# Moving a denominator row into the first of seven matrix products, and two products and two weight loads forward

## The chip, the cores and the metric

The kernel runs on one core of one Trainium2 chip. The metric is the device time of one execution in microseconds (us); lower is better. A core has TensorE (matrix products; PE in the profile, its weight loads PEld), VectorE (DVE), ScalarE (ACT) and GpSimd (POOL), each with an instruction queue of its own, and SyncE (SP), whose queue here issues the transfers (DMA) between the large memory (HBM) and the on-chip memory (SBUF). Matrix products land in PSUM, of which this kernel uses eight banks of 128 x 512 float32. Engines wait for one another by semaphores, which the kernel's framework derives from what each instruction reads and writes.

## The reference

Four layers, each with a residual: linear attention (A), a gated product (B), and both again with the same weights. S is 2048, D is 1024, 32 heads of 32.

```python
def _A_ref(x, wqkv, wo):
    qkv = (x @ wqkv) ...                       # q, k, v by head
    phi = lambda t: jnp.where(t > 0, t + 1, jnp.exp(t)) + 1e-6
    pq, pk = phi(q), phi(k)
    kv = jnp.einsum("bhsd,bhse->bhde", pk, v)
    z = jnp.einsum("bhsd->bhd", pk)            # sum of phi(k) over the sequence
    num = jnp.einsum("bhqd,bhde->bhqe", pq, kv)
    den = jnp.einsum("bhqd,bhd->bhq", pq, z)[..., None] + 1e-6
    o = num / den
    return o ... @ wo

x = x + _A_ref(_layernorm(x), A_wqkv, A_wo)    # layer 0
x = x + _B_ref(_layernorm(x), ...)             # layer 1
x = x + _A_ref(_layernorm(x), A_wqkv, A_wo)    # layer 2: the change is here
x = x + _B_ref(_layernorm(x), ...)             # layer 3
```

## The kernel before

Only the second attention (layer 2) is concerned. The kernel never forms v. It takes M = xn^T phi(k), a 1024 x 1024 product over the sequence (xn is the normalised x), and then kv = Wv^T M by head. M is done with seven products of blocks of half the size instead of eight (a Strassen-like scheme), each of four groups of eight matmuls, one group to a PSUM bank. X, Y and V are the banks; `done(j)` follows group j.

```python
def m_products(q_first):
    X = [self.ps.tile([P, NW], F32, tag="a", ...) for j in range(QT)]     # four banks
    Y = [self.ps3.tile([P, NW], F32, tag="b", ...) for j in range(2)]     # two banks
    Y += [self.kvp.tile([P, NW], F32, tag=f"kv{j}", ...) for j in range(2)]   # kv0, kv1
    mt, V, M5 = [], [], []

    def product(A, B, banks, start, done):
        for j in range(QT):
            for i in range(NS):
                nc.tensor.matmul(banks[j], lhsT=A(i)[:, j * P:(j + 1) * P], rhs=B(i), ...)
            done(j)
            later.tick()
    ...
    def add(out, j):                                     # VectorE
        nc.vector.tensor_tensor(out=out, in0=Y[j], in1=M5[j], op=ALU.add)

    product(..., X, True, lambda j: copy(Y[j], X[j]))    # 1: X, copied to Y by ScalarE
    mt += [self.slot(f"mt{l}_{h}", [P, 4, D]) for h in range(2)]
    product(..., X, False, evict(X, 0, 0))               # 2: X ends
    z_row()
    later.at(2, lambda: z_chain(0))
    V += [self.ps.tile([P, NW], F32, tag="a", ...) for j in range(QT)]
    for i in range(NS):
        later.at(1 + i // 2, lambda i=i: sums_last(i))
    product(..., V, True, keep)                          # 3
    product(..., Y, False, lambda j: add(V[j], j))       # 4: V starts from Y + M5
    product(..., V, False, evict(V, 0, 1))               # 5
    product(..., Y, False, lambda j: add(half(mt[1][:, j, :], 1), j))   # 6: M's second half
    kv.extend(self.ps.tile([P, NW], F32, tag="a", ...) for i in range(H))

    def steps(h, b):                                     # 16 matmuls of kv[b]
        for j in range(QT):
            kv_half(h * QT + j, mt[h][:, j, :], b)

    def last(j):
        copy(half(mt[1][:, j, :], 0), Y[j])
        if j < 3:
            steps(*((0, 1), (1, 1), (0, 0))[j])
        if j == 1:
            ring.load_to(ring.index((l, "o0")) + 1)      # half of wo

    product(..., Y, False, last)                         # 7
    q_first()
    later.tick()
    steps(1, 0)
    ring.load_to(ring.index((l, "o1")) + 1)              # other half of wo
    finish_kv()                                          # kv[0] by VectorE, kv[1] by ScalarE
# (cut: operands of the products)
```

`sums_last` makes, on VectorE, two in-place differences per row block (sixteen in all) which products 5 and 7 read, and which may be written only once product 2 has read the old values. The denominator: GpSimd sums phi(k) over row blocks into `ksum`; a matmul with ones then sums over the 128 rows (`z_row`); and each of sixteen row blocks of phi(q) is divided, by GpSimd and VectorE in turn:

```python
def z_row():
    hi = self.temp([P, D], BF16)
    nc.scalar.activation(out=hi, in_=ksum, func=ACT.Copy)
    for i in range(H):
        ps = self.ps.tile([P, NW], F32, tag="a")
        nc.tensor.matmul(ps, lhsT=self.ones, rhs=hi[:, i * NW:(i + 1) * NW], start=True, stop=True)
        nc.scalar.activation(out=zrow[:, i * NW:(i + 1) * NW], in_=ps, func=ACT.Copy)

def z_chain(i):
    z_mult(*divmod(i, QT))
    if i < 10:
        later.at(2, lambda: z_chain(i + 1))

def z_mult(sc, j):
    prod = ksum                                          # the one buffer of all products
    nc.gpsimd.tensor_tensor(out=prod, in0=pq_of[sc, j], in1=zrow, op=ALU.mult)
    later.at(2, lambda: z_sum(prod, sc, j))

def z_sum(prod, sc, j):
    nc.vector.tensor_reduce(out=den, in_=heads(prod), ...)
    nc.vector.tensor_scalar(out=den, in0=den, scalar1=1e-6, ...)
    nc.vector.reciprocal(out=den, in_=den)
    later.at(2, lambda: z_scale(den, sc, j))

def z_scale(den, sc, j):
    nc.gpsimd.tensor_tensor(out=heads(pq), in0=heads(pq), in1=den ..., op=ALU.mult)
    self.last_turn = nc.sync.dma_start_transpose(out=pqT[sc][:, :, j * P:(j + 1) * P], in_=pq)
# (cut)
```

`later.at(n, f)` runs f, that is, puts its instructions into the queues, n ticks later; a tick is a group or a unit of TensorE's work. `ring` is the list of weight tiles in order of use; `load_to` issues loads up to one of them, into a buffer that the pool has free. Weights, phi(q), its transposes and M's parts share one pool of sixteen buffers. After the products come the last quarter of q (units of eight matmuls, with phi by ScalarE and VectorE), four times `fold_wo` between them (kv times half of wo, which gives T), and the output units, T times the transposed phi(q).

Of the kernel before, what the change touches and what calls it, by code (L numbers as in the profile page):

```python
# [9 lines left out]
ACT = mybir.ActivationFunctionType  # L10
F32 = mybir.dt.float32
BF16 = mybir.dt.bfloat16
F16 = mybir.dt.float16
PSUM = bass.MemoryType.PSUM
P = 128
NW = 512
# [73 lines left out]
class _Net:  # L90
# [318 lines left out]
    def layer_A(self, l, last_ln):  # L409
        nc, G, KT, D = self.nc, self.G, self.KT, self.D  # L410
        ring, later = self.ring, self.later
        H = D // NW
        heads = lambda a: a.rearrange("p (h d) -> p h d", d=HD)
        pq_of, pqT, T = {}, {}, []
        kv = [] if l else [self.kvp.tile([P, NW], F32, tag=f"kv{i}", name=f"kv{l}_{i}")
                           for i in range(H)]
        kvc = self.slot(f"kvc{l}", [P, 4, D])
# [2 lines left out]
        ksum = kvc[:, 2:4, :].rearrange("p a d -> p (a d)").bitcast(F32)  # L420
# [33 lines left out]
            else:  # L454
                nc.gpsimd.tensor_tensor(out=ksum[:, cols], in0=ksum[:, cols], in1=pk, op=ALU.add)  # L455

        def z_row():

            hi = self.temp([P, D], BF16)
            nc.scalar.activation(out=hi, in_=ksum, func=ACT.Copy)  # L460
            for i in range(H):
                ps = self.ps.tile([P, NW], F32, tag="a")
                nc.tensor.matmul(ps, lhsT=self.ones, rhs=hi[:, i * NW:(i + 1) * NW],
                                 start=True, stop=True)
                nc.scalar.activation(out=zrow[:, i * NW:(i + 1) * NW], in_=ps, func=ACT.Copy)
# [17 lines left out]
        def kv_half(d, mt, b):  # L483
            for i in range(NW // P):
                nc.tensor.matmul(kv[b][:, i * P:(i + 1) * P].rearrange("p (i d) -> p i d", d=HD),
                                 lhsT=ring.get((l, f"v{b}"))[:, d, i * P:(i + 1) * P],
                                 rhs=by_row(mt[:, b * NW:(b + 1) * NW])[:, :, i, :], start=(d == 0 and i == 0),
                                 stop=(d == KT - 1 and i == NW // P - 1),
                                 skip_group_check=True)
# [8 lines left out]
        half = lambda a, n: a[:, n * NW:(n + 1) * NW]  # L498
# [16 lines left out]
        def sums_last(i):  # L515
            a, b = self.xn[l, self.NS + i], self.pk[l, self.NS + i]
            sub(half(a, 0).bitcast(F16), half(a, 0), part(i, 1))
            sub(half(b, 0).bitcast(F16), half(b, 0), part(i, 3))

        def m_products(q_first):  # L520

            NS = self.NS
            xn, pk = (lambda i: self.xn[l, i]), (lambda i: self.pk[l, i])
            f16 = lambda a: a.bitcast(F16)
            copy = lambda out, src: nc.scalar.activation(out=out, in_=src, func=ACT.Copy)
            X = [self.ps.tile([P, NW], F32, tag="a", name=f"mx{j}") for j in range(QT)]
            Y = [self.ps3.tile([P, NW], F32, tag="b", name=f"my{j}") for j in range(2)]
            Y += [self.kvp.tile([P, NW], F32, tag=f"kv{j}", name=f"my{2 + j}") for j in range(2)]
            mt, V, M5 = [], [], []

            def product(A, B, banks, start, done):
                for j in range(QT):
                    for i in range(NS):
                        nc.tensor.matmul(banks[j], lhsT=A(i)[:, j * P:(j + 1) * P], rhs=B(i),
                                         start=start and i == 0, stop=i == NS - 1,
                                         skip_group_check=True)
                    done(j)
                    later.tick()

            def evict(banks, h, n):  # L540
                return lambda j: copy(half(mt[h][:, j, :], n), banks[j])

            def keep(j):
                M5.append(self.temp(name="m5"))
                copy(M5[j], V[j])

            def add(out, j):
                nc.vector.tensor_tensor(out=out, in0=Y[j], in1=M5[j], op=ALU.add)

            product(lambda i: half(xn(i), 0), lambda i: half(pk(i), 0), X, True,  # L550
                    lambda j: copy(Y[j], X[j]))
            mt += [self.slot(f"mt{l}_{h}", [P, 4, D]) for h in range(2)]
            product(lambda i: half(xn(NS + i), 0), lambda i: half(pk(NS + i), 0), X, False,
                    evict(X, 0, 0))
            z_row()
            later.at(2, lambda: z_chain(0))
            V += [self.ps.tile([P, NW], F32, tag="a", name=f"mv{j}") for j in range(QT)]
            for i in range(NS):
                later.at(1 + i // 2, lambda i=i: sums_last(i))
            product(lambda i: part(i, 0), lambda i: part(i, 2), V, True, keep)  # L560
            product(lambda i: part(i, 1), lambda i: part(i, 3), Y, False, lambda j: add(V[j], j))
            product(lambda i: f16(half(xn(NS + i), 0)), lambda i: half(pk(NS + i), 1), V, False,
                    evict(V, 0, 1))
            product(lambda i: f16(half(xn(i), 1)), lambda i: f16(half(pk(i), 1)), Y, False,
                    lambda j: add(half(mt[1][:, j, :], 1), j))
            kv.extend(self.ps.tile([P, NW], F32, tag="a", name=f"kv{l}_{i}") for i in range(H))

            def steps(h, b):
                for j in range(QT):
                    kv_half(h * QT + j, mt[h][:, j, :], b)  # L570

            def last(j):
                copy(half(mt[1][:, j, :], 0), Y[j])
                if j < 3:
                    steps(*((0, 1), (1, 1), (0, 0))[j])
                if j == 1:
                    ring.load_to(ring.index((l, "o0")) + 1)

            product(lambda i: half(xn(NS + i), 1), lambda i: f16(half(pk(NS + i), 0)), Y, False, last)
            q_first()  # L580
            later.tick()
            steps(1, 0)
            ring.load_to(ring.index((l, "o1")) + 1)
            finish_kv()

        def finish_kv():
            n = NW // P
            nc.vector.tensor_copy(out=kvT[:, 0:n, :].rearrange("p g e -> p (g e)"), in_=kv[0])
            nc.scalar.activation(out=kvT[:, n:2 * n, :].rearrange("p g e -> p (g e)"), in_=kv[1],
                                 func=ACT.Copy)  # L590
# [12 lines left out]
# [6 lines that stand above are left out]
            prod = ksum  # L609
            nc.gpsimd.tensor_tensor(out=prod, in0=pq_of[sc, j], in1=zrow, op=ALU.mult)  # L610
            later.at(2, lambda: z_sum(prod, sc, j))
# [70 lines left out]
        if l == 0:  # L682
            steps = self.head()
# [29 lines left out]
        with self.tc.manual_schedule(engines={mybir.EngineType.DVE, mybir.EngineType.Pool}):  # L713
            q3 = row_major(q_unit, self.NQ - 1)
            out0 = column_major(out_unit, 0)
            if l == 0:
                ring.free_before((l, "v0"))
                later.at(5, z_row)
                later.at(7, lambda: z_chain(0))
                for d in range(KT):  # L720
                    m_units(d)
            else:
                ring.load_to(ring.index((l, "v1")) + 1)
                m_products(q3.pop(0))
                q3.insert(0, lambda: None)
                later.at(1, lambda: self.behind(ring.last, self.bring_back, range(self.NS)))
                for t in range(self.NS, self.ST, 2):
                    later.at(10 + t, lambda t=t: self.behind(self.last_turn, self.bring_back, (t, t + 1)))
# [334 lines left out]
```

## Time and profile before

| what | value |
|---|---|
| time, median of 3 runs | 1488.01 us (1485.56 to 1488.08) |
| span of the profiled execution | 1483.2 us |
| granted TensorE clock, mean | 0.999 |
| products 1 to 7 of layer 2, TensorE | 841.33 to about 894.8 us from the span's start |
| last quarter of q and the folds | about 893 to 916.8 us |
| output units of layer 2 | about 914.8 to 972 us |

A row of the profile's groups names the source line, the engine, the operation, what it writes and reads, and its times. L534 is a matmul of a product, L463 the matmul with ones, L485 one of kv, L641 of a fold, L436 of a projection, L656 of an output unit. On VectorE, L500 is a difference, L548 the sum `add`, L615 to L617 the reduce, the added 1e-6 and the reciprocal of a denominator, L383 and L385 phi, L588 the copy of kv[0], L650 a copy of a fold. On GpSimd, L455 is the sum into `ksum`, L610 the multiply of a denominator, L622 its scale. On ScalarE, L460 is the copy of `ksum`, L465 that of the row. In a view in order of time the columns are start and duration in us, engine, line, operation, output and inputs, and the count of merged instructions; what stands in brackets is how long the engine had been idle before it, and what ended that.

### The profile page before, as it was taken

How to read it: one execution, taken by the hardware profiler on the slowest of the kernel's cores; microseconds unless marked ns; L12 is line 12 of the kernel's file. 1: busy time of each engine (PE TensorE's matmuls, PEld its weight loads, DVE VectorE, ACT ScalarE, POOL GpSimd, SP SyncE). 2: the span in 40 equal slices, each digit the busy share in tenths (PEclk: the TensorE clock that was granted, in tenths of full speed). 3: DMA queues.
4: the chain of work that ended last, by engine and by line, in shares of the span. 5: the costliest groups of instructions: out<-in, count | busy, mean ns of one | idle time of the engine just before them, and what ended most of it. 6: DMA issues, size and time to landing. Idle time of an engine off the chain costs nothing.

```text
span 1483.2 us, 18604 instructions
## 1 busy us (share of the span) xinstructions
PE 1468.9 (99%) x6965; PEld 667.1 (45%) x7007; DVE 873.1 (59%) x1495; ACT 512.8 (35%) x919; POOL 284.0 (19%) x190
## 2 busy tenths in 40 slices
PE   9999999999999999999999998999999999999999
PEld 4444444444444444444444444444444444444444
DVE  8995787666594434455379867874445433434632
ACT  5752323333330333340067523343333203333300
POOL 1356540111100011110023485401111000111000
PEclk9999999999999999999999999999999999999999
DMA  9855538444458954446833029894444688444461
GB/s 280 220 167 177 114 59 246 156 143 156 161 185 251 338 179 131 148 131 199 251 100 71 1 39 293 213 279 142 138 145 131 187 244 268 142 142 146 150 209 43
DMA packets 316059, 251.32 MB, mean 169 GB/s; under 512 B 105536, under 2 KB 291136, under 8 KB 315072
## 3 DMA queue, kind: packets, MB, share of 16 engines
q1 hardware_dynamic: 306000, 229.80, 52.6%
q10 hardware_dynamic: 9968, 20.32, 3.7%
q8 instruction: 55, 0.90, 0.3%
q14 instruction: 36, 0.29, 0.1%
HBM read 190.84 MB, written 34.60 MB: 152 GB/s over the span
## 4 chain that ended last, share of the span: by engine, by line
PE 91%; DVE 6%; POOL 2%; DMA 1%; issue 1%; ACT 0%; DVEq 0%
PE ps L436 14%; PE yg L850 10%; PE dy L934 10%; PE yu L850 10%; PE dv L934 6%; PE dx L934 6%; PE xg L850 6%; PE xu L850 6%; PE ps L473 4%; PE vg L850 3%; PE vu L850 3%; PE zu L850 3%; PE zg L850 3%; PE ps L656 3%; DVE x L663 1%; DVE stats L154 1%
## 5 line engine op out<-in xcount | busy, mean ns | idle before, releaser
L850 PEld LDWEIGHTS <-w 128*128 128x128 f16 (+1 forms) x3136 | 306.3, 98 | 371.3 <-DVE w L788 1.1
L888 POOL TENSOR_TENSOR h<-m5u,m5g 128x512 f16<-128x512 f32 x56 | 71.2, 1271 | 812.1 <-DVE m5u L884 801.2
L436 PE MATMUL ps<-w,xnT 128*128 128x512 bf16 x1024 | 224.8, 381 | 0.2 <-ACT xnT L296 0.2
L934 PEld LDWEIGHTS <-h 128*128 128x128 f16 x1120 | 109.4, 98 | 132.3
L881 DVE TENSOR_TENSOR zg<-yg,m5g 128x512 f32<-128x512 f32 x56 | 39.2, 699 | 203.5 <-PE yg L850 203.5
L436 PEld LDWEIGHTS <-xnT 128*128 128x128 bf16 x1024 | 99.6, 98 | 121.3 <-issue 3.5
L850 PE MATMUL yg<-s,w 128*128 128x512 f16 x448 | 115.2, 380 | 0.0
L850 PE MATMUL xu<-xnT,w 128*128 128x512 f16 x448 | 115.0, 380 | 0.0
L850 PE MATMUL xg<-xnT,w 128*128 128x512 f16 x448 | 115.0, 380 | 0.0
L850 PE MATMUL yu<-s,w 128*128 128x512 f16 x448 | 115.0, 380 | 0.0
L656 PE MATMUL ps<-T,pqT 128*128 128x512 bf16 x500 | 110.5, 380 | 2.7 <-DVE x L663 2.1
L858 ACT ACTIVATE m5g<-m5g 128x512 f32<-128x512 f32 x56 | 35.2, 629 | 200.2 <-DVE m5g L884 200.2
L934 PE MATMUL dy<-w,h 128*128 128x512 f16 x448 | 98.0, 380 | 0.0
L934 PE MATMUL dx<-w,h 128*128 128x512 bf16 x436 | 96.7, 379 | 0.6
L610 POOL TENSOR_TENSOR kvc<-pq,kvc 128x1024 f32<-128x1024 bf16 x32 | 70.4, 2200 | 71.9 <-DVE den L615 57.7
L656 PEld LDWEIGHTS <-pqT 128*128 128x128 bf16 x512 | 49.9, 98 | 62.9 <-issue 3.1
L154 DVE BATCH_NORM_STATS2 stats<-x 128x6 f32<-128x512 f32 (+1 forms) x120 | 76.6, 672 | 0.5 <-DMA x<-in_A_x_dram 0.3
L161 ACT ACTIVATE rstd<-mv,eps 128x1 f32<-128x1 f32 x64 | 18.1, 289 | 162.2 <-DVE mv L159 162.1
L455 POOL TENSOR_TENSOR kvc<-kvc,slab 128x512 f32<-128x512 f32 x46 | 58.3, 1273 | 73.7 <-DVE slab L385 56.0
L861 DVE TENSOR_TENSOR h<-yu,r 128x512 f16<-128x512 f32 x56 | 38.7, 691 | 56.6 <-PE yu L850 56.6
L884 DVE TENSOR_TENSOR m5u<-yu,m5u 128x512 f32<-128x512 f32 x56 | 38.7, 692 | 54.0 <-PE yu L850 54.0
L934 PEld LDWEIGHTS <-e 128*128 128x128 f16 x448 | 43.8, 98 | 52.9
(127 smaller groups left out, 1969.6 us busy)
## 6 DMA issues: line engine op xcount, KB each, us to landing
w<-in_B_W_gate_dram SPq DMA_DIRECT2D x56, 512.0 KB, 6.0
w<-in_B_W_up_dram SPq DMA_DIRECT2D x56, 512.0 KB, 4.8
w<-td SPq DMA_DIRECT2D x32, 896.0 KB, 4.8
w<-in_B_W_down_dram SPq DMA_DIRECT2D x24, 896.0 KB, 5.4
w<-tg SPq DMA_DIRECT2D x42, 512.0 KB, 7.0
w<-tu SPq DMA_DIRECT2D x42, 512.0 KB, 5.6
w<-in_A_wqkv_dram SPq DMA_DIRECT2D x10, 1024.0 KB, 7.8
away<-x SPq DMA_DIRECT2D x16, 512.0 KB, 4.0
```

The source lines that it names most:

```text
L154: self.nc.vector.bn_stats(out=stats[:, c, :], in_=src[:, c * fmax:(c + 1) * fmax])
L436: nc.tensor.matmul(by_row(ps), lhsT=self.xnT[l, l_q][:, kt, j * P:(j + 1) * P], rhs=w[:, kt, :].rearrange("p (b i d) -> p i b d", i=R, d=H ...
L455: nc.gpsimd.tensor_tensor(out=ksum[:, cols], in0=ksum[:, cols], in1=pk, op=ALU.add)
L473: nc.tensor.matmul(ps, lhsT=self.xn[l, t][:, d * P:(d + 1) * P], rhs=self.pk[l, t][:, h * NW:(h + 1) * NW], start=(t == 0), stop=(t == sel ...
L610: nc.gpsimd.tensor_tensor(out=prod, in0=pq_of[sc, j], in1=zrow, op=ALU.mult)
L656: nc.tensor.matmul(ps, lhsT=pqT[sc][:, g, j * P:(j + 1) * P], rhs=T[g // 4][:, g % 4, n2 * NW:(n2 + 1) * NW], start=(g == 0), stop=(g == G ...
L850: nc.tensor.matmul(ps, lhsT=W[w][m][:, k, :], rhs=A[m][:, k, :], start=start and k == 0, stop=k == 3, skip_group_check=True)
L861: self.last_put = nc.vector.tensor_tensor(out=h[:, b, :], in0=ps, in1=R.pop(b), op=ALU.mult)
L881: nc.vector.tensor_tensor(out=Z[w], in0=Y[w], in1=V[w], op=ALU.add)
L884: nc.vector.tensor_tensor(out=V[w], in0=Y[w], in1=V[w], op=ALU.add)
L888: nc.gpsimd.tensor_tensor(out=h[:, 3, :], in0=V["u"], in1=V["g"], op=ALU.mult)
L934: nc.tensor.matmul(banks[j], lhsT=A(k)[:, j * P:(j + 1) * P], rhs=w[:, i, :], start=start and k == 0, stop=k == self.U - 1, skip_group_che ...
```

## The change

The row of denominators is made earlier: its two matmuls follow the third and the fourth group of product 1 and use the bank kv1, which product 1 otherwise needs only for its fourth copy. It is for starting the divisions of phi(q) sooner. The value products of M's second half with the second half of v's weights (`steps(1, 1)`) follow the first group of product 7 instead of the second, `steps(0, 0)` the second instead of the third, and the loads of wo's halves are asked for after groups 1 and 2 of product 7 instead of after group 2 and at the end.

```diff
-        def z_row():
+        def z_row(halves=range(H), pool=self.ps, tag="a"):
 
-            hi = self.temp([P, D], BF16)
-            nc.scalar.activation(out=hi, in_=ksum, func=ACT.Copy)
-            for i in range(H):
-                ps = self.ps.tile([P, NW], F32, tag="a")
+            if 0 in halves:
+                hi_of.append(self.temp([P, D], BF16))
+                nc.scalar.activation(out=hi_of[0], in_=ksum, func=ACT.Copy)
+            hi = hi_of[0]
+            for i in halves:
+                ps = pool.tile([P, NW], F32, tag=tag)
                 nc.tensor.matmul(ps, lhsT=self.ones, rhs=hi[:, i * NW:(i + 1) * NW],
 ...
-            Y += [self.kvp.tile([P, NW], F32, tag=f"kv{j}", name=f"my{2 + j}") for j in range(2)]
+            Y += [self.kvp.tile([P, NW], F32, tag="kv0", name="my2")]
 ...
-            product(lambda i: half(xn(i), 0), lambda i: half(pk(i), 0), X, True,
-                    lambda j: copy(Y[j], X[j]))
+            def seed(j):
+                if j >= 2:
+                    z_row((j - 2,), self.kvp, "kv1")
+                if j == 3:
+                    Y.append(self.kvp.tile([P, NW], F32, tag="kv1", name="my3"))
+                    later.at(2, lambda: z_chain(0))
+                copy(Y[j], X[j])
+
+            product(lambda i: half(xn(i), 0), lambda i: half(pk(i), 0), X, True, seed)
             mt += [self.slot(f"mt{l}_{h}", [P, 4, D]) for h in range(2)]
             product(lambda i: half(xn(NS + i), 0), lambda i: half(pk(NS + i), 0), X, False,
                     evict(X, 0, 0))
-            z_row()
-            later.at(2, lambda: z_chain(0))
 ...
                 copy(half(mt[1][:, j, :], 0), Y[j])
-                if j < 3:
-                    steps(*((0, 1), (1, 1), (0, 0))[j])
-                if j == 1:
-                    ring.load_to(ring.index((l, "o0")) + 1)
+                if j == 0:
+                    steps(0, 1)
+                    steps(1, 1)
+                elif j == 1:
+                    steps(0, 0)
+                if j < 2:
+                    ring.load_to(ring.index((l, f"o{j}")) + 1)
 ...
             steps(1, 0)
-            ring.load_to(ring.index((l, "o1")) + 1)
             finish_kv()
```

(Cut: the new list `hi_of`, and unchanged lines.)

## The prediction

> **What bounds the kernel now.** I read the page first (busy shares, then the chain that ended last), then TensorE's waits, then the order of time around the seven products, one engine at a time.
>
> ```profile
> PE 1468.9 (99%) x6965; PEld 667.1 (45%) x7007; DVE 873.1 (59%) x1495; ACT 512.8 (35%) x919; POOL 284.0 (19%) x190
> ```
>
> TensorE is busy for 1468.9 of 1483.2 us. A change that leaves its matmuls as they are can move the time only through the 14.3 us in which it isn't. The waits name what of that lies near the change (engine, line waited for, us in total, times, longest):
>
> ```profile
> PE fold L641 <- DVE T L650: 3.1, 1, 3.1
> PE ps L656 <- DVE x L663: 2.1, 2, 1.3
> PE idle L246 <- DVE e L243: 1.3, 1, 1.3
> PE fold L641 <- DVE kvc L588: 0.6, 1, 0.6
> ```
>
> The first and last lie just after the products. Together 3.65 us (3.05 and 0.60 in order of time), and that is all the change can win there. TensorE in order of time (start, us, what, count, [idle before]):
>
> ```profile
> 846.78 0.38 PE L534 MATMUL mx<-x,xn 128*128 128x512 bf16 x1
> ...
> 855.41 0.59 PE L463 MATMUL ps<-e,ones 128*128 128x512 bf16 x2
> 855.84 7.07 PE L534 MATMUL mv<-x 128*128 128x512 f16 x32
> ...
> 887.82 1.06 PE L485 MATMUL kv<-mt,w 128*128 128x128 bf16 x16
> ...
> 899.89 0.44 PE L641 MATMUL fold<-w,kvc 32*32 32x512 bf16 x16 [0.60 <-DVE kvc L588]
> 900.26 3.63 PE L436 MATMUL ps<-w,xnT 128*128 128x512 bf16 x16
> 906.94 0.66 PE L641 MATMUL fold<-w,kvc 32*32 32x512 bf16 x16 [3.05 <-DVE T L650]
> ```
>
> To be seen: the fourth group of product 1 starts at 846.78, the denominator row (L463) stands between products 2 and 3, and no wait falls inside the products. The other engines there:
>
> ```profile
> 847.68 1.06 ACT L460 ACTIVATE e<-kvc 128x1024 bf16<-128x1024 f32 x1 [3.84 <-POOL kvc L455]
> ```
>
> ```profile
> 854.10 5.46 DVE L500 TENSOR_TENSOR slab<-slab,x 128x512 f16<-128x512 bf16 x16 [6.17 <-PE mx L534]
> ...
> 878.43 1.22 DVE L615 TENSOR_REDUCE den<-kvc 128x32 f32<-128x1024 f32 x1 [1.69 <-POOL kvc L610]
> 879.68 0.62 DVE L616 TENSOR_SCALAR den<-den 128x32 f32<-128x32 f32 x1
> ...
> 896.42 2.02 DVE L383 TENSOR_SCALAR e<-e 128x512 f32<-128x512 f32 x1
> ```
>
> ```profile
> 857.33 4.21 POOL L610 TENSOR_TENSOR kvc<-pq,kvc 128x1024 f32<-128x1024 bf16 x1 [9.68 <-ACT kvc L465]
> ...
> 876.28 2.11 POOL L610 TENSOR_TENSOR kvc<-pq,kvc 128x1024 f32<-128x1024 bf16 x1
> 878.36 1.90 POOL L622 TENSOR_TENSOR pq<-pq,den 128x1024 bf16<-128x1024 bf16 x1
> ```
>
> Two things: the bf16 copy of the key sums, which the row needs, ends only at 847.68 + 1.06 = 848.74. And GpSimd and VectorE shut each other out: the first multiply takes 4.21 instead of 2.11 us because VectorE's sixteen subtractions run until 859.56, and L383 takes 2.02 us under a GpSimd multiply, where its rows near 836 to 845 in the same view have 0.41 to 0.42.
>
> **What the skill says.** "SBUF — State Buffer", section "Who interferes with whom", says that a GpSimd instruction and a VectorE one with two SBUF inputs, or in a two-port mode, hold one port pair exclusively, the second to come blocking; a reduce never contends. The trace agrees: 4.21 against 2.11 us, and the reduce L615 takes 1.22 us under a running multiply. "PSUM — Partial Sum Buffer", section "Engine vs sequencer instructions", says that the VectorE, ScalarE and GpSimd queues are strict FIFO and matmuls start in program order; so a denominator placed ahead of a subtraction on VectorE holds it up. Here the sums that start or end a product's bank (L548) indeed alternate with the reduces L615 in program order.
>
> **The change, part by part.** No instruction is added or dropped; matmul counts are equal. What moves is the order.
>
> Row of denominators. Its halves now follow the third and fourth group of product 1. The first half stands in TensorE's queue where 846.78 is now, and waits for the copy that ends at 848.74 (nothing ahead of it changes): 2.0 us of new idleness. The two row matmuls cost 0.43 us in either place (855.41 to 855.84). So product 3 starts near 857.85 instead of 855.84. ScalarE has the second half copied at about 848.8 + 0.22 + 1.73 + 1.0 = 851.8, so the first GpSimd multiply starts at 851.9, 5.4 us sooner than 857.33.
>
> VectorE's order. Denominators 1 and 2 now stand ahead of the sixteen subtractions, number 3 after twelve of them, number 4 after the first product-4 sum; mt's last sum stands behind denominator 9 (it stood behind 6). Each denominator is multiply 2.1 (GpSimd), reduce 1.25, then add and reciprocal (0.55, or about 1.0 under a GpSimd instruction), scale 1.9 (GpSimd); undisturbed, GpSimd repeats each 3.95 us (876.28 to 880.23). Working it through: multiply 1 ends 854.0, reduce 855.25; multiply 2 ends 857.45, reduce 858.7; scale 1 ends 859.3; multiply 3 ends 861.4. The twelve subtractions take the ports then, 12 x 0.34 = 4.1, to 865.5. Reduce 3 ends 866.7; GpSimd's scale 2, shut out until 865.4, ends 867.3; multiply 4 ends 869.4. Four subtractions to 870.8; first product-4 sum 871.5; reduce 4 at 872.7; second and third sum 873.7 and 874.3; multiply 5 ends 874.8; denominator 5 with its reciprocal 877.0; fourth sum 877.7.
> Product 5 would start its four groups at 871.65, 873.4, 875.1 and 876.8. It waits about 0.35 for the second sum and 0.5 for the fourth: 0.85 us. It ends at 879.5, product 6 at 886.4.
>
> Value products. Those of the second half with v1 (the second of the four sixteens of L485) now follow the first group of product 7 instead of the second. They need all four sums of mt's second half. Going on at 3.95 us from multiply 6 (876.6), multiply 9 ends at 890.55, its denominator at 892.8, the fourth sum at 893.45. TensorE has done the first group of product 7 and the first sixteen at 886.4 + 1.73 + 0.9 = 889.05, and twelve more small matmuls at 889.7. It waits about 3.8 us. In the kernel before that sum was done by 884.56 + 1.22 = 885.8, before anyone asked.
>
> What is won. All eleven denominators now stand ahead of the phi of the last quarter on VectorE, and the eleventh is done near 900.6, while the key-value product of the first half ends near 902.5 on the shifted clock. So L588 is done at 904.2, before the fold would start (906.1), and L383 no longer waits behind GpSimd: both fold waits go, 3.65 us.
>
> Weights. The loads of wo stand earlier in the program but not on their queue: the first now takes the buffer of the second quarter of phi(q), so it stands behind four transposes (before: three), and must wait for the last to land. Scale 8 ends at 892.4, its transpose lands 3.1 later (its median), the load takes 5.7 to 7.2 (the two loads' range): 901.3 to 902.8, as against a fold at 906.1. The second load follows scale 11 (902.5): issue 903.9, landed 909.6 to 911.1, needed at about 913.9. Hidden, nothing won, some 3 us to spare.
>
> Sum on TensorE: 2.0 + 0.85 + 3.8 - 3.65 = +3.0 us. The second fold check: 906.1 + 0.36 + 3.5 = 909.95 instead of 906.94, again +3.0. What follows (output units, 1.35 us wait at 961) moves along.
>
> **Rivals.** First, VectorE and GpSimd take turns differently: if the ports pass freely during the twelve subtractions, multiply 9 ends near 888 and the fourth sum near 890.5. The waits for value products and product 5 then sum to about 0.9, and the total is 2.0 + 0.9 - 3.65 = -0.8 us, 1487.2. Against it stands the 4.21 us multiply, which waited for a whole train. Second, the intended effect alone: the row's early start hides everything and the folds' waits go: -3.65, 1484.4. Against it stands 848.74: the row can't start when its place comes. Third, a late weight load: should the second wo load take 10.3 us (the longest of such loads in the kernel), it lands at 914.2, some 0.3 us late; with its issue held up too, 1 to 2 us. That gives 1492 to 1493. Fourth, TensorE's clock: the skill, "TensorE: Matmul & The Clock Gate", section "What's actually happening", says the clock halves after an idle window of about 3.4 us. My longest wait is 3.8. Before, a 3.05 us wait was followed by fold matmuls of up to 605 instead of 385 ns, while the granted clock stayed 0.999 over the span. A window at half clock would lose about 1.7 us, my estimate from that page: 1492.7.
>
> **Range and chances.** From 1488.01, the main line gives 1491.0. The first rival has perhaps a quarter of my belief, the late additions a fifth, so I set 1490.5. The three runs before spread over 2.5 us. Range 1486.5 to 1494. Two per cent would be 29.8 us; TensorE has only 14.3 us of idleness to give, and nothing puts more than some 8 us on its path: 0.01, 0.98, 0.01.
>
> **What would show it.** Right: a wait of about 2 us of the first row matmul on ScalarE's copy near 846.8; the first GpSimd multiply near 852 and about 2.1 us long; GpSimd's scale 2 stretched to near 6 us; a wait of 3 to 4 us of a value product on VectorE's sum near 890; no wait at the folds. Wrong: no wait at the row; the value products' wait under 1 us (then the time falls below 1488); a fold waiting on a weight load or still on VectorE; or a stretch of slow matmuls after a wait.

## The result and the profile after

| | before | after |
|---|---|---|
| time, median of 6 runs each | 1486.76 us (1485.56 to 1488.08) | 1492.38 us (1491.30 to 1493.93) |
| ratio, 95% interval | | 1.0039 [1.0026, 1.0051] |
| span of the profiled execution | 1483.2 us | 1491.9 us |
| first matmul of product 1 to the last fold | 841.33 to 916.39: 75.06 us | 842.38 to 922.98: 80.60 us |

The change costs 5.6 us. The stretch from product 1 to the last fold is 5.54 us longer, so that is where to look. (The profiled span is 8.7 us longer: 1.05 of the rest lie ahead of product 1 and 2.1 behind the last fold, where an output unit waited 1.97 us instead of 1.35 and ran slowly after it. The times differ by 5.6, so this is left out below.) Line numbers have moved: L536 is a matmul of a product, L465 the matmul with ones, L487 one of kv, L650 of a fold, L665 of an output unit, L502 a difference, L550 the sum `add`, L624 the reduce of a denominator, L619 the multiply on GpSimd and L631 its scale.

TensorE's waits in the changed kernel (engine, line waited for, us in total, times, longest):

```profile
PE kv L487 <- DVE mt L550: 3.4, 3, 3.0
PE mv L536 <- DVE mv L550: 3.0, 3, 2.3
PE ps L665 <- DVE x L672: 2.8, 2, 2.0
PE ps L465 <- ACT e L461: 1.8, 1, 1.8
```

Both waits at the folds are gone, as intended. Three stand in their place: the row (L465) for ScalarE's copy of the key sums, product 5 (`mv`) for the sums that start its banks, the value products (`kv`) for mt's last sum. In order of time on TensorE (start, us, what, count, [idle before]):

```profile
875.13 1.89 PE L536 MATMUL mv<-slab 128*128 128x512 bf16 x7 [2.26 <-DVE mv L550]
877.44 3.61 PE L536 MATMUL mv<-slab 128*128 128x512 bf16 x16 [0.43 <-DVE mv L550]
881.34 1.89 PE L536 MATMUL mv<-slab 128*128 128x512 bf16 x8 [0.28 <-DVE mv L550]
...
897.09 0.38 PE L487 MATMUL kv<-mt,w 128*128 128x128 bf16 x4 [2.98 <-DVE mt L550]
897.31 2.73 PE L536 MATMUL my<-slab 128*128 128x512 f16 x8
899.84 1.91 PE L487 MATMUL kv<-mt,w 128*128 128x128 bf16 x16
```

To be seen: 2.26 us at the start of product 5, where none was foretold. And after the 2.98 us wait eight matmuls take 2.73 us and sixteen small ones 1.91, where the same groups take 1.89 and 1.06 elsewhere: TensorE runs slow for a while. The table by stretches confirms it (stretch, length, TensorE's busy time, granted clock, DMA share, GB/s); first the changed kernel:

```profile
897.00:901.60 4.60, 4.51 (x29) 0.63 0.50 120
```

and the same table of the kernel before, after its 3.05 us wait at the fold:

```profile
906.90:911.00 4.10, 4.06 (x26) 0.58 1.01 402
```

A clock of 0.63 over 4.60 us is 1.7 us lost; 0.58 over 4.10 is the same. The kernel before had paid for its long wait twice as well, in the wait and in slow matmuls, and the change got both back.

Why product 5 waits stands on the other two engines. VectorE, then GpSimd, in the changed kernel:

```profile
860.71 7.42 DVE L502 TENSOR_TENSOR slab<-slab,x 128x512 f16<-128x512 bf16 x12
...
869.79 4.68 DVE L502 TENSOR_TENSOR slab<-slab,x 128x512 f16<-128x512 bf16 x4
...
896.41 0.63 DVE L550 TENSOR_TENSOR mt<-my,m 128x512 bf16<-128x512 f32 x1
```

```profile
860.33 2.12 POOL L619 TENSOR_TENSOR kvc<-pq,kvc 128x1024 f32<-128x1024 bf16 x1
862.41 2.09 POOL L631 TENSOR_TENSOR pq<-pq,den 128x1024 bf16<-128x1024 bf16 x1
869.35 2.12 POOL L619 TENSOR_TENSOR kvc<-pq,kvc 128x1024 f32<-128x1024 bf16 x1 [4.85 <-DVE den L624]
```

The sixteen differences took 5.46 us in one piece before; now twelve take 7.42 and four 4.68. GpSimd's multiply and the scale behind it take 2.12 and 2.09 us (a scale alone 1.90), so they run from 860.33 to 864.5 almost undisturbed, and the differences wait for both. The first two of the twelve, each by itself:

```profile
860.71 2.02 DVE L502 TENSOR_TENSOR slab<-slab,x 128x512 f16<-128x512 bf16 x1
862.65 2.13 DVE L502 TENSOR_TENSOR slab<-slab,x 128x512 f16<-128x512 bf16 x1
```

The first waits for the multiply and passes when it has ended (862.45); the second, which begins after the scale has begun (862.41), waits for the scale. The other ten then take 3.43 us together.

TensorE's stretches, from these and the same rows of the kernel before, add up (product 6 takes 6.91 us in both; the last stretch ends where the last fold starts):

| stretch on TensorE | before | after | change |
|---|---|---|---|
| product 1 to start of product 4 | 21.42 | 23.42 | +2.00 |
| start of product 4 to start of product 6 | 13.81 | 17.26 | +3.45 |
| product 7 with its value products | 9.59 | 15.07 | +5.48 |
| last quarter of q with the folds | 23.33 | 17.94 | -5.39 |
| sum | | | +5.54 |

The first of these is the row's wait (1.84, and 0.16 for the restart: the first matmul after a wait takes 0.38 us, where one in a row follows the one before it after 0.22), the second product 5's three waits and restarts, the third the value products' three with the slow matmuls, the last what was won at the folds.

### The profile page after: what moved, and what is told of

The parts are those of the page before. It is cut to its first block, busy times and chain, and to the rows that moved or that the text cites. A ratio compares the mean times of both kernels' runs of the same rounds, so it can differ in the third digit from the quotient of the medians.

```text
span 1491.9 us, 18613 instructions
## 1 busy us (share of the span) xinstructions
PE 1472.4 (99%) x6965; PEld 669.5 (45%) x7007; DVE 876.1 (59%) x1495; ACT 512.8 (34%) x919; POOL 281.7 (19%) x190
## 4 chain that ended last, share of the span: by engine, by line
PE 83%; DVE 7%; POOL 2%; issue 1%; DMA 1%; ACT 0%; DVEq 0%; POOLq 0%
PE yg L859 10%; PE dy L943 10%; PE yu L859 10%; PE ps L436 8%; PE dv L943 6%; PE dx L943 6%; PE xg L859 6%; PE xu L859 6%; PE ps L475 3%; PE vg L859 3%; PE vu L859 3%; PE zu L859 3%; PE zg L859 3%; PE ps L665 3%; DVE x L672 1%
## 5 line engine op out<-in xcount | busy, mean ns | idle before, releaser
L665 PE MATMUL ps<-T,pqT 128*128 128x512 bf16 x500 | 112.2, 383 | 3.4 <-DVE x L672 2.8
L619 POOL TENSOR_TENSOR kvc<-pq,kvc 128x1024 f32<-128x1024 bf16 x32 | 68.0, 2126 | 82.7 <-DVE den L624 74.0
L665 PEld LDWEIGHTS <-pqT 128*128 128x128 bf16 x512 | 50.3, 99 | 64.8 <-issue 6.1
```

Source lines behind the costliest of these rows:

```text
L665: nc.tensor.matmul(ps, lhsT=pqT[sc][:, g, j * P:(j + 1) * P], rhs=T[g // 4][:, g % 4, n2 * NW:(n2 + 1) * NW], start=(g == 0), stop=(g == G ...
```

## The experiments

Under "stretch" stands the time from product 1's first matmul to the last fold in the run's profile; time and ratio are against the kernel before on the same chip.

| run | time - before, us | ratio, 95% interval | stretch, us |
|---|---|---|---|
| before | | | 75.06 |
| the change (again, beside the others) | +5.5 | 1.0036 [1.0023, 1.0049] | 80.60 |
| row alone | +8.0 | 1.0053 [1.0041, 1.0065] | 82.72 |
| value products and loads alone | +0.2 | 1.0000 [0.9992, 1.0008] | 76.21 |
| change, value products late | +0.9 | 1.0005 [0.9997, 1.0013] | 75.91 |
| change, row one group later | +4.4 | 1.0030 [1.0018, 1.0042] | 79.21 |
| change, chain later | +2.2 | 1.0016 [1.0009, 1.0022] | 77.13 |
| change, filler matmuls in the wait | +5.7 | 1.0034 [1.0022, 1.0047] | 78.93 |
| change, two scales later | +4.2 | 1.0027 [1.0017, 1.0037] | 78.57 |
| change, pause in the chain | +3.2 | 1.0024 [1.0015, 1.0032] | 79.50 |
| before, chain of nine | -3.6 | 0.9979 [0.9970, 0.9987] | 69.67 |
| before, chain of nine, late ones denser (products overwritten) | -3.7 | 0.9974 [0.9964, 0.9984] | 69.66 |
| before, chain of nine, late ones denser | -3.8 | 0.9976 [0.9965, 0.9986] | 69.66 |

### The change again

No edit.

> The changed kernel once more beside the two, for its time and for which of its waits come again in another execution: +5.6 us against before as measured; the waits of product 5 (about 3.4), of the value products (about 3) and of the row (1.8) again if they follow from the order of the instructions; the half clock after the value products' wait may or may not come again.

The waits came again to 0.02 us (2.26, 0.42, 0.29; 2.97; 1.84), with the stretch of 80.60 and the slow matmuls behind the value products' wait. So they are not the chance of one execution.

### Each part alone

The row alone is the part of the diff above that touches `z_row`, `Y` and product 1, applied to the kernel before.

> The kernel before with the early row alone; value products and loads of wo where they were. Theory 1: row wait 2.0, product 5 late by 3.4, the value products, now after the second group of product 7, still wait about 2.3 us for VectorE's last sum. The first load of wo then stands behind the tenth scale's transpose on its queue and lands near 911 to 912, where the first fold could start near 908: a wait of 3 to 4.5 us in place of the two fold waits won. In all +6 to +8 us against before, so the early row needs the earlier loads. Theory 2 (the moved value products are the loss): +1 us or less.

The value products and loads alone are the rest of it:

```diff
-                if j < 3:
-                    steps(*((0, 1), (1, 1), (0, 0))[j])
-                if j == 1:
-                    ring.load_to(ring.index((l, "o0")) + 1)
+                if j == 0:
+                    steps(0, 1)
+                    steps(1, 1)
+                elif j == 1:
+                    steps(0, 0)
+                if j < 2:
+                    ring.load_to(ring.index((l, f"o{j}")) + 1)
```

> The kernel before with the earlier value products and earlier loads of wo alone; the row where it was. Theory 1: VectorE's last sum of M's second half is ready at 885.8, just before it is asked for at 886.7, and the loads keep their place among the transposes: no difference, -0.5 to +0.7 us. Theory 2 (value products directly after the first group disturb ScalarE's or TensorE's order by themselves): +3 us or more, as in the changed kernel.

The row by itself loses more than the whole change, +8.0; the other part is worth nothing by itself, +0.2, and the folds wait 3.1 and 0.6 us as before. The parts don't add up, since 8.0 + 0.2 is more than 5.6. With the row alone the value products wait 1.3 us, not the 2.3 expected, and a fold waits as expected:

```profile
PE fold L648 <- DMA w<-in_A_wo_dram: 3.7, 1, 3.7
```

(The fold waits for a transfer of wo.) Its first load of wo is issued at 905.43, behind the transposes of phi(q) in SyncE's queue, more of them since the denominators come earlier. In the whole change that load is issued at 899.24, ahead of two of these, and no fold waits for it. Before, it was issued at 893.48. So the earlier request made no load earlier than it had been; it kept the early denominators' transposes from pushing it past its need.

### The value products late again

```diff
-                if j == 0:
-                    steps(0, 1)
-                    steps(1, 1)
-                elif j == 1:
-                    steps(0, 0)
+                if j < 3:
+                    steps(*((0, 1), (0, 0), (1, 1))[j])
```

> The changed kernel, with the value products of M's second half with v's second weights moved from the first to the third group of product 7 (steps(0,0) follows the second); all else as changed. Theory 1 (the time is lost to sums of the VectorE that stand behind denominators, and to TensorE's clock after the wait): the wait of 3.35 us and the half-clock stretch behind it (1.65 us) go, some 2.4 us of it come back as a wait of the first fold for the copy of kv[0], since VectorE's phi then meets GpSimd's eleventh scale: about -3.0 us against the changed kernel, 1489 to 1490. Theory 2 (the placement of the value products is harmless, the early row is all): no difference over 0.5 us. Theory 3 (the late load of wo bounds this stage): the wait moves to the first fold in full, no gain.

It came to +0.9, not +2.6: the value products' wait is gone, and the fold wait of 2.4 that was expected in its place did not appear. Product 5 still pays. Its first wait is 2.26 us as in the change, but here its matmuls then ran slowly, so that the two small waits behind it had no room to show (the stretch of product 5, its length, TensorE's busy time, granted clock, DMA share, GB/s):

```profile
874.49:883.24 8.75, 8.75 (x33) 0.80 0.27 51
```

Product 5 takes 8.59 us from its first matmul to product 6 here (874.49 to 883.08), and 7.93 in the change (875.13 to 883.06).

### The row one group later

```diff
             def seed(j):
-                if j >= 2:
-                    z_row((j - 2,), self.kvp, "kv1")
                 if j == 3:
-                    Y.append(self.kvp.tile([P, NW], F32, tag="kv1", name="my3"))
+                    z_row((0,), self.kvp, "kv1")
                     later.at(2, lambda: z_chain(0))
-                copy(Y[j], X[j])
+                else:
+                    copy(Y[j], X[j])
 ...  # second half, and the fourth copy, after the first group of product 2
```

> The changed kernel, with the row's first half after the fourth group of product 1 and its second half after the first group of product 2, so that the wait of 1.84 us for ScalarE's copy of the key sums shrinks to about 0.3. Theory 1 (what sets product 5's start is the chain copy, row, first multiply, denominators, VectorE's sums, and not TensorE): the row is complete at the same time, so product 5 waits 1.7 us longer and the time is unchanged, or up to 1.7 us longer if that longer wait lets the clock drop. Theory 2 (each TensorE wait is a cost of its own): -1.7 us.

TensorE's waits in this run:

```profile
PE mv L536 <- DVE mv L550: 4.3, 1, 4.3
PE kv L487 <- DVE mt L550: 3.0, 1, 3.0
```

The row no longer waits, and product 5's first wait grows from 2.26 to 4.26, by the 2.0 us that the row had held TensorE. So the row's wait cost nothing of its own here: VectorE's sums were the later ones in any case. The time is 1.1 us below the change's, and the intervals overlap; whether the row's place is worth anything is not decided by them.

### The chain later, the row early

```diff
-                    later.at(2, lambda: z_chain(0))
+                    later.at(7, lambda: z_chain(0))
```

> The changed kernel, with the chain of denominators put into the queues five ticks later, so that VectorE's order is as in the kernel before (all sixteen differences ahead of the first denominator); the row stays early. Theory 1: product 5 waits no more (-3.4), the value products wait no more (-5.0), the row's wait stays (+2.0 against before) and both fold waits are back (+5.4 with their half-clock stretch): 2.0 us above the kernel before, about -3.5 us against the changed one. Theory 2 (the row's place costs the time): as the changed kernel, +5 to +6 against before.

This puts the chain where the kernel before had it and leaves the row in product 1. The row waits 1.84, the folds 3.05 and 0.58 again, product 5 and the value products nothing: +2.2 us, and a stretch 2.07 us longer. That is the row's term alone. It also shows that product 5's wait and the value products' come from the chain's place and not from the row's.

### Two scales later: who goes first at the shared port

```diff
-            later.at(2, lambda: z_scale(den, sc, j))
+            later.at(7 if l and (sc, j) in ((0, 1), (0, 2)) else 2,
+                     lambda: z_scale(den, sc, j))
```

> The changed kernel with the scales of the second and third row of tiles made five ticks later, nothing else moved: GpSimd then has no scale queued behind its second and third multiply while VectorE makes the differences for products 4 and 5. Theory (GpSimd's queued instruction goes ahead of a queued train of VectorE differences at the shared port): the twelve differences that took 7.42 us take about 5.8 or less, the four that took 4.68 about 3, and the wait of product 5 (2.3 + 0.43 + 0.28 and the latencies, 3.4 in all) falls below 1.5. As the two scales have to be made later, among the sums, the value products' wait of 3.0 stays or grows; so the time falls by 0 to 2 us against the changed kernel, +3.5 to +5.5 against before. Rival (the differences are late because the chain of denominators in VectorE's own order is, not for the port): the twelve differences still take about 7.4 us and product 5 waits as in the changed kernel.

VectorE and then TensorE in this run:

```profile
860.28 5.71 DVE L502 TENSOR_TENSOR slab<-slab,x 128x512 f16<-128x512 bf16 x12
...
867.64 2.96 DVE L502 TENSOR_TENSOR slab<-slab,x 128x512 f16<-128x512 bf16 x4
...
889.36 0.69 DVE L550 TENSOR_TENSOR mt<-my,m 128x512 bf16<-128x512 f32 x1 [2.77 <-DMA pqT<-pq]
```

```profile
890.11 3.28 PE L536 MATMUL my<-slab 128*128 128x512 f16 x8 [3.84 <-DVE mt L550]
```

With one GpSimd instruction in their way instead of two, the differences take 1.71 and 1.72 us less (a scale alone is 1.9), and product 5 waits for nothing. The rival falls. But the work was only put off: by the profile VectorE idles 2.77 us ahead of mt's first sum for a transpose of phi(q), which a late scale holds up. (Phi(q) and mt take their buffers from one pool; that this is why the sum waits for a transpose was not tested.) Product 7 waits 3.84 us for its bank, and eight slow matmuls come after it (3.28 instead of 1.89). The value products still wait 2.0. The stretch gains 2.0 of the 3.4 us.

### A pause in the chain

```diff
-                later.at(2, lambda: z_chain(i + 1))
+                later.at(8 if l and i == 5 else 2, lambda: z_chain(i + 1))
```

> The changed kernel with a pause in the chain: after the sixth denominator the next waits eight ticks instead of two, so that three denominators no longer stand ahead of mt's sums in VectorE's order but among the folds; the value products stay where the change put them. Theory (the value products wait because the denominators, at GpSimd's pace of nearly 4 us each, stand ahead of mt's sums): the wait of 3.0 and the half clock behind it go, the waits of product 5 (2.3 and two small ones) and of the row (1.8) stay, and what comes back is at most a fold or output unit that waits for the later denominators: +0.5 to +3 us against before. Rival (mt's sums are late because product 5 is, whatever stands between): the value products still wait 2 us or more, +4 to +6 us.

The value products' wait and the slow matmuls behind it are gone; the waits of the row and of product 5 are the same to 0.01 us. From product 1 to the last quarter of q it is 57.15 us (841.20 to 898.35), in the change 62.66 (842.38 to 905.04): 5.5 us won, what the stretch of product 7 had lost. The three denominators then stand between the phi and the copies of the folds on VectorE, and the last quarter, to the last fold, takes 22.35 us instead of 17.94, with these new waits of TensorE:

```profile
PE ps L436 <- DVE pq L385: 0.8, 1, 0.8
PE fold L650 <- DVE T L659: 0.5, 1, 0.5
```

These two waits are 1.2 of the 4.4 us. Some 0.65 is no loss, since ten matmuls of output units run ahead of the last fold here and seven in the change; the rest was not taken apart. The rival, that product 5's delay is what makes mt's sums late, falls.

### Filler matmuls in the value products' wait

The changed kernel with twelve matmuls more between the two value products, so that TensorE is not idle there.

> The changed kernel with twelve matmuls more, with ones, into a spare bank that nothing reads, between the two value products after the first group of product 7: 2.6 us of work laid into the 3.35 us wait. Theory 1 (TensorE's clock halves for one window after the wait, and that costs 1.65 us): TensorE is not idle long enough, the half-clock stretch goes, -1.65 us against the changed kernel in spite of the added work. Theory 2 (the slow matmuls behind the wait come from something else, as transfers or queue refill): 0, or a loss of up to 0.5 us.

TensorE in order of time (L585 is the filler):

```profile
893.33 2.75 PE L585 MATMUL spare<-slab,ones 128*128 128x512 bf16 x12
...
897.18 0.38 PE L487 MATMUL kv<-mt,w 128*128 128x128 bf16 x4 [0.42 <-DVE mt L550]
```

The wait shrinks to 0.42 and the matmuls after it run at full clock; the stretch is 1.67 us shorter than the change's. The time isn't: in the profiled run product 5 ran slowly after its wait (clock 0.81 from 875.00 to 884.00), and an output unit waited 2.92 us and was slow after it. So the slow matmuls do follow the idleness, but by filling one gap nothing measurable was won in the time.

### A shorter chain in the kernel before

If the folds wait because eleven denominators stand ahead of the last phi, two fewer should do what the early row was for, without moving the row.

```diff
-            if i < 10:
+            if i < (8 if l else 10):
                 later.at(2, lambda: z_chain(i + 1))
 ...
-            for i in range(11, self.ST):
-                later.at(1 + 3 * (i - 11), lambda i=i: z_mult(*divmod(i, QT)))
+            n = 9 if l else 11
+            for i in range(n, self.ST):
+                later.at(1 + 3 * (i - n), lambda i=i: z_mult(*divmod(i, QT)))
```

> The kernel before with the chain of denominators ended after nine in place of eleven; the other two are made with the last five among the output units. Theory 1 (the folds wait because phi on VectorE stands behind denominators ten and eleven and is shut out by GpSimd's multiplies): both fold waits and the half-clock stretch go, -5.4 us against before, about 1481.4. Rival: VectorE is full among the output units, and what is won comes back there as waits of TensorE: -1 to -3 us.

-3.6 us, between the two. No wait from product 1 to the last fold is left, and the stretch is 5.39 us shorter than before, just what the change had won there: Theory 1 holds for the folds. As the rival has it, some comes back at the output units, which wait 2.9 us in all for VectorE's additions and 1.1 for a transpose (1.35 in all before).

The late denominators every second tick (`1 + 2 * (i - n)`): in this order each late product but the last is overwritten before its sum is made, so six row blocks get the next block's denominator. The instructions are the same in number and size.

> The kernel before with the chain of the second attention ended after nine denominators, and the seven late ones every second tick among the output units instead of every third. Theory: what kept the every-third version at -3.6 instead of -5.4 us is that the last transposes and sums come late for the output units; sooner late denominators take that wait back: -4 to -5.4 us against before, the output units' waits back at about 1.35 us. Rival: the output units wait for VectorE's sums, which closer denominators hold up more: -2 to -3.6 us, their waits 2.5 us or more.

The same with each sum ahead of the next product:

```diff
+            if i < (8 if l else 10) or (l and 9 <= i < self.ST - 1):
+                later.at(2, lambda: z_chain(i + 1))
 ...
+            if l:
+                later.at(1, lambda: z_chain(9))
```

> The kernel before with the chain ended after nine denominators, the seven late ones in a chain of their own, one every second tick, each sum ahead of the next product: as fast as the every-third version or a little faster, -3.5 to -4.5 us against before, the output units' waits about 2.7 us in all. Rival: denser denominators hold VectorE's additions for the output units up more: -2 to -3 us, waits over 3.5 us.

TensorE's wait at the output units, of this last run:

```profile
PE ps L656 <- DVE x L663: 3.0, 3, 1.3
```

The transpose is waited for no more, the additions for about as long as with every third tick (2.9), and the time is -3.8, as expected and not the -2 to -3 of the rival. The overwritten version came to -3.7 with waits of 2.7 us in layer 2: not the -4 to -5.4 of its theory, and nearly what its rival said. The intervals of the three versions overlap. This last version beats both kernels.

## Why the prediction was right or wrong

The time, 1492.38, lies in the range of 1486.5 to 1494 and within 2%. But the predicted time was 1490.5, its main line +3.0 us, and the stretch shows +5.5: a range of 7.5 us covers a miss of 2.5, and that the time lies in it does not make every step right. By its own steps:

| step | predicted | measured |
|---|---|---|
| row waits for ScalarE's copy | +2.0 | +2.0 |
| product 5 waits for the sums | +0.85 | +3.45 (2.97 of waits, the rest restarts) |
| value products wait for mt's last sum | +3.8 | +3.83 (3.35 of waits, the rest restarts) |
| TensorE slow after that wait (fourth rival) | +1.7, not in the main line | +1.65 |
| fold waits go | -3.65 | -3.65, and -1.74 of slow matmuls and restarts behind them |
| sum | +3.0 | +5.54 |

*Row of denominators:* right, place, releaser and size. The chain moved later alone left +2.2 us. That in the change itself the row's wait is no separate cost (a row one group later gives it all to product 5) the sum did not say.

*VectorE's order:* this is the step that failed. The order within each queue was as worked out, and so was the wait for the running multiply, which ended at 861.40 on the clock of the kernel before (predicted 861.4); who gets the shared port next was not. From the 4.21 us multiply of the kernel before, "which waited for a whole train", the prediction let all twelve differences pass ahead of GpSimd's scale 2, "shut out until 865.4" and so near 6 us long. Scale 2 took 2.09 us, from 862.41: one difference passed ahead of it, and the other eleven waited. Scale 3 met the four in the same way. From the end of the multiply the two trains took 5.7 and 3.0 us where 4.1 and 1.4 were set down. Taking the scales away took 1.7 us from each, which shows it. In the kernel before VectorE's train had begun at 854.10, when GpSimd had nothing to do, and the multiply came in its midst; here the multiply was running when the first difference came. Why a GpSimd instruction does not get in between two differences of a running train is not shown. The first product-4 sum ended at about 875.1 instead of 871.5 (872.55 with the later start of 1.05 us), and product 5 lost 2.6 us more than predicted. That is the whole difference between +3.0 and +5.5.

*Value products:* right in cause and nearly in size, 3.35 us of waits and 3.83 with the restarts (15.07 - 9.59 - 1.65), though both sides of it came 2.5 us later than worked out: mt's last sum ended at 895.99 on the clock of before (predicted 893.45), and product 7 began at 888.92 (predicted 886.4). The pause shows that the denominators ahead of the sums cause it.

*What is won:* the two waits went, as foretold. Mis-sized: a fold wait of 3.05 us had cost 1.6 more in slow matmuls, 1.74 with the restarts, so 3.65 was not "all the change can win there". The prediction had seen those (605 instead of 385 ns) but priced them only for a wait to come, in the fourth rival, and not for the wait removed. By chance the two, +1.65 and -1.74, cancel.

*Weights:* hidden, as foretold: issued at 899.24 and 907.80, no fold waits. "Nothing won" is only half true: with the row early and the loads not asked for sooner, a fold waits 3.7 us.

*Rivals:* the first (ports pass freely) and the second (only the intended effect) fall with the three new waits; the third (a late second load of wo) was not there in the change; the row alone meets a late first load. The fourth came true, and with it one of the signs that the prediction had named for being wrong, slow matmuls after a wait. Its signs for being right all came but the stretched scale 2, the value products' wait (2.98 us at the longest) some 3 us later than worked out.

*A reading:* the reduce of 1.22 us that the prediction puts under a running multiply runs under a scale (878.36 to 880.26 in its own lines); nothing hangs on it.

## What to carry to other kernels

Starting a chain of small operations sooner also puts it ahead of what others wait for, in every in-order queue it passes through; before moving it, list for each consumer what stands ahead of its input afterwards. Here the wait at the end of the chain was removed more cheaply by cutting two links from it (-3.6 us) than by starting it five us sooner (+5.6 us). Price a wait of some 3 us on TensorE with the slow matmuls that can follow it (here up to 1.7 us, once 2.6), both where it is made and where it is taken away.

## What the runs showed of the hardware

*Who gets the shared port next.* The Trainium skill, "SBUF — State Buffer", section "Who interferes with whom", has the second to come blocked. The traces agree for one instruction against one, and show more for queues. A GpSimd multiply that came when VectorE's train of sixteen differences was running got in between no two of them: it took 4.21 us instead of 2.1 and ended 1.98 us after the train. Where a multiply was running first, one waiting difference passed after it, then the scale that GpSimd had queued, and then the other eleven differences (7.42 us with two GpSimd instructions in the way, 5.71 with one, 4.1 by the rate of the undisturbed sixteen).

*Slow matmuls after short waits.* The same skill's "TensorE: Matmul & The Clock Gate", section "What's actually happening", names an idle window of about 3.4 us before the clock halves. Here less was enough. The traces' record of the granted clock has half clock in stretches of 3.41 us (once 6.83), and where one execution has several, they begin whole multiples of 3.41 us apart (897.60 and 969.28 in the change again, 875.48 and 913.03 with the row alone), so the time is cut into fixed windows (these are 21 and 11 of them apart). The windows around the value products' wait, which is 2.98 us in both runs (window, length, TensorE's busy time, granted clock, DMA share, GB/s), in the change:

```profile
894.80:898.21 3.41, 1.12 (x9) 1.00 0.30 56
898.21:901.62 3.41, 3.41 (x22) 0.50 0.39 108
```

and with the row one group later:

```profile
892.27:895.68 3.41, 1.55 (x28) 1.00 0.41 77
895.68:899.09 3.41, 2.29 (x19) 1.00 0.41 77
```

In the change 2.29 us of the idleness lie in one window, and the next is at half clock; in the other run a border cuts the wait into 1.86 and 1.12, and no half clock follows. In all fourteen profiled executions, the first and last few us aside, half clock began after each window with 1.97 us of idleness or more, fourteen times, and after none with 1.95 or less. Each wait of 3.05 us or more here left that much in one window and was followed by half clock (3.05 three times, 3.72, 3.84, 4.26); the row's 1.84 never was. The first wait of product 5, 2.25 to 2.27 us, lay in one window in three runs (value products late, filler, row alone), where half clock followed, and was cut in three others (the change twice, the pause), where it did not. A stretch lost 1.4 to 1.7 us; the one of 6.83, with the value products and loads alone, lost 2.6 (sixteen matmuls in 6.18 us instead of 3.63), which is most of why that run's stretch is 1.15 us over before's. There a border cut the wait of 3.05 us into 2.03 and 1.03, and the half clock went on after the second part.
